# First four chunks of batch 0's q and k: from casting loads on GpSimd's queue to float32 loads on SyncE's queue with casts on chip

## The chip, the cores and the metric

The kernel runs on one core of a Trainium2 chip. The metric is device time in microseconds (us) of one execution. Before the change three runs took 257.55, 257.65 and 257.77 us (median 257.65). Shorter is better.

A core has a matmul engine (TensorE, PE in the profile), a vector engine (VectorE, DVE), an activation engine (ScalarE, ACT), GpSimd (POOL) and SyncE (SP). Sixteen DMA engines move data between memory and the core's on-chip buffer; SP, ACT and POOL issue to them, each through a queue of its own (in the profile q0 "software_dynamic" is POOL's, q1 SP's, q10 ACT's).

## The reference, cut to what matters

```python
qn = q / (np.linalg.norm(q, axis=1, keepdims=True) + 1e-06)      # q, k, v: 4 x 6400 x 256, float32
kn = k / (np.linalg.norm(k, axis=1, keepdims=True) + 1e-06)
s = kn.transpose(0, 2, 1) @ qn / tau                             # 256 x 256 for each batch
a = softmax(s)                                                   # over the last axis
x = v @ a                                                        # 25600 x 256
logits = x @ w_gate                                              # 8 experts, the best two of a row kept
out = x + sum over the two experts e of  w_e * (x @ A[e]) @ B[e] # rank 16
```

q, k, v and the output have 26.2 MB each. w_gate (8 KB), A (128 KB) and B (128 KB) are called the constants here.

## The kernel before, in words

For each of the 4 batches the kernel forms the 256 x 256 product of k and q ("gram", L194) and the sums of squares ("norm", L206, over squares made at L184 on ACT and L186 on DVE); a chain of seven short steps (`chain0` to `chain6`, L213 to L297) makes the softmax from them; then v is transposed and run through the softmax, the gate and the experts (L315 to L479). Batch 0's gram runs alone at the start (L491 to L500), then batch 0's chain (L501). From there one loop (L530 on) works in slots of two 128-row chunks of v, and the grams of batches 1 to 3 are dealt out over its slots. Each engine takes its instructions in the order written; nothing is rescheduled.

A batch has 50 chunks of 128 rows. q and k come in tiles `qk` of 10 chunks each (PC = 10, 4 buffers), v in tiles `vt` of 18, 16 and 16 chunks (3 buffers). All are loaded by POOL (L137, L138, L140), and these loads turn float32 into bfloat16 on the way. One partition's share of a 10-chunk load is 10 KB of float32 in one piece, so a load is 128 pieces, 8 for each of the 16 DMA engines. `load_more` (L119) issues the loads of a sorted list until the next tile's buffer is still in use; its argument limits how many tiles it takes. Before the gram it is called at L152 (three tiles), then the two identity matrices are made on POOL (L153 to L156), then at L163 (which gets one more tile, after which the four buffers are taken). The fifth tile of batch 0 comes in two parts, of 6 and 4 chunks.

SP loads the constants first (L149 w_gate, L150 A, L151 B; `wst`, `ast`, `bst`, float32). DVE casts them to bfloat16 at L168 to L171, before anything else that it does but three memsets. They are first used by batch 0's `chain5` (`wg_sb`, `A_sb`) and much later by L470 (`ball_sb`). SP has no other work until the last part of the kernel; most output is stored through ACT's queue (L488) out of tiles `ys`, of which there are 8 in rotation (L473).

The steps of the chain that the prediction touches, for batch 0: `chain2` ends with two multiplications on DVE (L243), `chain3` is the exponential on ACT (L251), `chain4` transposes it on PE (L263) and copies it out on DVE (L267), `chain5` multiplies it with the constants on PE (L279, L281).

Of the kernel before, what the change touches and what calls it, by code (L numbers as in the profile page):

```python
# [8 lines left out]
FP32 = mybir.dt.float32  # L9
BF16 = mybir.dt.bfloat16  # L10
# [6 lines left out]
def kernel(  # L17
# [16 lines left out]
    nc = tc.nc  # L34
    B, N, C = q.shape
    P = 128
    NC = N // P
    CC = C // P
    E = moe_w_gate.shape[1]
    R = moe_A.shape[2]  # L40
# [4 lines left out]
    PC = 10  # L45
    NPAIR = NC // 2
    NPT = B * NPAIR
    GRP = 5
    QKB, VB, YB = 4, 3, 8
    VP = [18, 16, 16]  # L50
    DEFER = 6

    GRAM = {1: (0, 20), 2: (24, 45), 3: (49, 67)}
# [2 lines left out]
    q_v = q.rearrange("b (p c) d -> b p c d", p=P)  # L56
    k_v = k.rearrange("b (p c) d -> b p c d", p=P)
# [3 lines left out]
    const = ctx.enter_context(tc.tile_pool(name="const", bufs=1))  # L61
# [4 lines left out]
    y_pool = ctx.enter_context(tc.tile_pool(name="yp", bufs=YB))  # L66
# [15 lines left out]
    for b, (first, last) in GRAM.items():  # L82
        n = last - first + 1
        for c in range(NC):
            s = first + c * n // NC
# [3 lines left out]

    loads = []  # L90
    for s in range(NC // PC):
        loads.append((-10 + s, "qk", 0, s, [PC] if s < NC // PC - 1 else [6, 4]))
        for b in range(1, B):
            loads.append((qk_need[b, s], "qk", b, s, [PC]))
    for b in range(B):
        for s, n in enumerate(VP):
            loads.append((NPAIR * b + sum(VP[:s]) // 2 + 1, "v", b, s,
                          [8, 4, 4] if b == B - 1 and s == len(VP) - 1 else [n]))
    loads.sort(key=lambda x: x[0])
    tiles = {"qk": {}, "v": {}}  # L100
    left = {"qk": [], "v": []}
# [4 lines left out]
    def piece(kind, c):  # L106
# [3 lines left out]
        s = 0  # L110
        while c >= VP[s]:
            c -= VP[s]
            s += 1
# [5 lines left out]
    def load_more(limit=1000):  # L119

        while limit and at_load[0] < len(loads):
            _, kind, b, s, parts = loads[at_load[0]]
            n = len(left[kind])
            if n >= bufs[kind] and left[kind][n - bufs[kind]]:
                return
            where[kind, b, s] = n
            left[kind].append(sum(parts))
            c0 = s * PC if kind == "qk" else sum(VP[:s])
            if kind == "qk":
                t = qk_pool.tile([P, 2, PC, C], BF16, tag="qk", name="qk")  # L130
            else:
                t = v_pool.tile([P, max(VP), C], BF16, tag="v", name="vt")
            tiles[kind][b, s] = t
            o = 0
            for m in parts:
                if kind == "qk":
                    nc.gpsimd.dma_start(t[:, 0, o:o + m, :], q_v[b, :, c0 + o:c0 + o + m, :])  # L137
                    nc.gpsimd.dma_start(t[:, 1, o:o + m, :], k_v[b, :, c0 + o:c0 + o + m, :])  # L138
                else:
                    nc.gpsimd.dma_start(t[:, o:o + m, :], v_v[b, :, c0 + o:c0 + o + m, :])  # L140
                o += m
            at_load[0] += 1
            limit -= 1


    wst = const.tile([P, CC * E], FP32)
    ast = const.tile([P, E, CC * R], FP32)
    bst = const.tile([P, C], FP32)
    nc.sync.dma_start(wst, moe_w_gate.rearrange("(p cc) e -> p (cc e)", p=P))  # L149
    nc.sync.dma_start(ast, moe_A.rearrange("e (p cc) r -> p e (cc r)", p=P))  # L150
    nc.sync.dma_start(bst, moe_B.rearrange("e r d -> (e r) d"))  # L151
    load_more(3)  # L152
    ident = const.tile([P, P], BF16)  # L153
    make_identity(nc, ident)
    ident_f = const.tile([P, P], FP32)
    make_identity(nc, ident_f)  # L156
    ones_bf = const.tile([P, 2], BF16)
    nc.vector.memset(ones_bf, 1.0)
    ones_f = const.tile([P, P], FP32)
    nc.vector.memset(ones_f, 1.0)  # L160
    neg_inv_tau = const.tile([P, 1], FP32)
    nc.vector.memset(neg_inv_tau, -inv_tau)
    load_more(3)  # L163

    wg_sb = const.tile([P, CC, E], BF16)
    A_sb = const.tile([P, CC, E, R], BF16)
    ball_sb = const.tile([P, C], BF16)
    nc.vector.tensor_copy(wg_sb.rearrange("p cc e -> p (cc e)"), wst)  # L168
    for cc in range(CC):
        nc.vector.tensor_copy(A_sb[:, cc, :, :], ast[:, :, cc * R:(cc + 1) * R])  # L170
    nc.vector.tensor_copy(ball_sb, bst)  # L171


    acc, nrm, sqs = {}, {}, {}
# [130 lines left out]
    for b in range(B):  # L305
        f = 0
# [174 lines left out]
    def send(keep):  # L481


        eng = nc.scalar if keep else nc.sync
        while len(unsent) > keep:
            gr = unsent.pop(0)
            c0, n = 2 * (gr["f"] - gr["b"] * NPAIR), 2 * gr["n"]
            eng.dma_start(out_v[gr["b"], :, c0:c0 + n, :], gr["ys"][:, 0:n, :])  # L488


    for c in range(0, NC, 2):  # L491
        square(0, c, "act" if (c // 2) % 2 else "dve")
        gram(0, c)
        gram(0, c + 1)
        load_more()
        if c >= 4:
            norm(0, c - 4)
            norm(0, c - 3)
    for c in range(NC - 4, NC):
        norm(0, c)  # L500
    for f, _ in CHAIN:  # L501
        f(0)

    def gram_part(items):
        for b, c in items:
            gram(b, c)
            if c >= 2:
                norm(b, c - 2)
            if c == NC - 1:
                norm(b, c - 1)  # L510
                norm(b, c)
# [18 lines left out]
    while nz < NPT or zq is not None or dq is not None:  # L530
# [4 lines left out]
        f, us, fb = (None, 0.0, 0) if behind else at_chain.get(slot, (None, 0.0, 0))  # L535
# [21 lines left out]
        dq, zq = zq, u  # L557
        send(max(0, min(DEFER, DEFER - (slot - GRAM[B - 1][1]) // 4)))
        if behind:
# [53 lines left out]
```

## Time and profile before

| | us |
|---|---|
| median of three runs | 257.65 |
| profiled execution, device time | 257.5 |
| its span in the profile | 255.7 |
| busy: PE / DVE / ACT / POOL | 215.5 / 150.6 / 174.9 / 30.9 |
| DMA: q0 (POOL's loads), time of its packets as a share of 16 engines' span | 75.3% |
| DMA: q10 (ACT's stores) / q1 (SP's) | 18.7% / 6.8% |
| read from memory / written | 78.91 MB / 26.21 MB |

The page cuts the span into 40 slices and gives each engine's busy tenths, the mean busy share of the DMA engines and what they moved. Its GB/s count bytes as they are written: a casting load writes half of what it reads, so 215 GB/s of q, k and v on chip are 430 GB/s read. The shares of DMA time add up the times of packets that overlap a little, so a full queue reads 1.03 to 1.1 and not 1.00. Other views used below: windows (busy time, DMA share and GB/s of chosen stretches), the timeline (instructions in order of time, with what ended the idle time before them in square brackets), the DMA view of a stretch (packets, MB and share of each queue), and the chain of waits that ended last.

### The profile page before, as it was taken

How to read it: one execution, taken by the hardware profiler on the slowest of the kernel's cores; microseconds unless marked ns; L12 is line 12 of the kernel's file. 1: busy time of each engine (PE TensorE's matmuls, PEld its weight loads, DVE VectorE, ACT ScalarE, POOL GpSimd, SP SyncE). 2: the span in 40 equal slices, each digit the busy share in tenths (PEclk: the TensorE clock that was granted, in tenths of full speed). 3: DMA queues.
4: the chain of work that ended last, by engine and by line, in shares of the span. 5: the costliest groups of instructions: out<-in, count | busy, mean ns of one | idle time of the engine just before them, and what ended most of it. 6: DMA issues, size and time to landing. Idle time of an engine off the chain costs nothing.

```text
span 255.7 us, 7679 instructions
## 1 busy us (share of the span) xinstructions
PE 215.5 (84%) x3256; PEld 191.1 (75%) x3256; DVE 150.6 (59%) x573; ACT 174.9 (68%) x288; POOL 30.9 (12%) x64
## 2 busy tenths in 40 slices
PE   0383884586899999999999989999899899999990
PEld 0262772475699987998999878989798789999970
DVE  1231333226386687775867857666577787777750
ACT  2333456449268778887888797887776877877881
POOL 8031131021012010210110202000000200000000
PEclk9997795589799999999999999999999999999998
DMA  7999999999999999999999999999999999999985
GB/s 122 219 214 214 211 215 219 210 216 215 214 218 213 220 209 216 216 214 214 215 218 210 288 269 289 218 307 256 284 261 269 372 342 352 383 424 425 421 368 210
DMA packets 12882, 66.29 MB, mean 259 GB/s; under 512 B 2480, under 2 KB 2608, under 8 KB 9008
## 3 DMA queue, kind: packets, MB, share of 16 engines
q0 software_dynamic: 8064, 39.33, 75.3%
q10 hardware_dynamic: 2160, 19.66, 18.7%
q1 hardware_dynamic: 2624, 6.82, 6.8%
q8 instruction: 25, 0.41, 0.6%
q14 instruction: 9, 0.07, 0.1%
HBM read 78.91 MB, written 26.21 MB: 411 GB/s over the span
## 4 chain that ended last, share of the span: by engine, by line
PE 47%; DMA 38%; DVE 7%; ACT 3%; issue 2%; POOL 1%; DVEq 0%; ACTq 0%; POOLq 0%
DMA qk<-in_k_dram 21%; PE y_ps L450 12%; DMA vt<-in_v_dram 11%; PE acc L194 8%; PE zg L434 6%; PE y_ps L470 6%; PE vT_ps L328 5%; DMA out_dram<-ys 5%; PE zg L458 3%; PE vT_ps L349 3%; PE nrm L206 3%; ACT sq L184 2%; DVE gz L438 2%; ACT ys L474 1%; DVE lm L384 1%
## 5 line engine op out<-in xcount | busy, mean ns | idle before, releaser
L184 ACT ACTIVATE sq<-qk 128x1024 bf16<-128x1024 bf16 x87 | 89.3, 1054 | 31.5 <-DMA qk<-in_k_dram 26.7
L194 PE MATMUL acc<-qk 128*128 128x256 bf16 x400 | 75.8, 292 | 19.9 <-DMA qk<-in_k_dram 19.9
L474 ACT COPY ys<-y_ps 128x512 f32<-128x512 f32 x100 | 58.7, 587 | 25.8 <-PE y_ps L470 21.8
L450 PE MATMUL y_ps<-a_bf,vT 128*128 128x256 bf16 x400 | 60.3, 273 | 0.3 <-ACT ys L474 0.3
L206 PEld LDWEIGHTS <-sq 128*128 128x128 bf16 x800 | 45.2, 99 | 8.5 <-ACT sq L184 3.1
L194 PEld LDWEIGHTS <-qk 128*128 128x128 bf16 x400 | 33.1, 102 | 23.7 <-DMA qk<-in_k_dram 20.8
L438 DVE TENSOR_TENSOR gz<-zg,gate 128x256 bf16<-128x256 f32 x100 | 41.6, 417 | 14.0 <-PE zg L434 12.4
L339 DVE COPY vT<-vT_ps 128x512 bf16<-128x512 bf16 x63 | 26.7, 423 | 34.3 <-PE vT_ps L328 33.6
L206 PE MATMUL nrm<-ones_bf,sq 128*128 128x1 bf16 x800 | 44.5, 165 | 1.2 <-ACT sq L184 1.2
L328 PE MATMUL vT_ps<-ident,vt 128*128 128x128 bf16 x400 | 39.5, 223 | 6.5 <-DMA vt<-in_v_dram 6.3
L434 PE MATMUL zg<-wa_sb,vT 128*128 128x128 bf16 x400 | 38.4, 218 | 1.2 <-DVE gzT L464 1.0
L470 PE MATMUL y_ps<-ball_sb,gzT 128*128 128x256 bf16 x200 | 38.4, 274 | 0.0
L328 PEld LDWEIGHTS <-vt 128*128 128x128 bf16 x400 | 29.9, 99 | 9.7 <-DMA vt<-in_v_dram 7.2
L450 PEld LDWEIGHTS <-vT 128*128 128x128 bf16 x400 | 33.5, 97 | 3.2 <-issue 0.4
L337 ACT COPY vT<-vT_ps 128x512 bf16<-128x512 bf16 x37 | 21.7, 587 | 10.2 <-PE vT_ps L328 8.7
L458 PE MATMUL zg<-ident,gz 128*128 128x128 bf16 x200 | 27.6, 220 | 1.1 <-DVE gz L438 0.6
L434 PEld LDWEIGHTS <-vT 128*128 128x128 bf16 x400 | 25.9, 96 | 3.4 <-issue 2.2
L464 DVE COPY gzT<-zg 128x256 bf16<-128x256 bf16 x90 | 25.2, 280 | 0.0
L137 POOL DMA_DIRECT2D qk<-in_q_dram x21 | 11.4, 542 | 111.8 <-ACT sq L184 31.8
L186 DVE TENSOR_TENSOR sq<-qk 128x1024 bf16<-128x1024 bf16 x13 | 8.9, 692 | 18.2 <-DMA qk<-in_k_dram 13.2
L458 PEld LDWEIGHTS <-gz 128*128 128x128 bf16 x200 | 15.0, 97 | 2.9 <-DVE gz L438 2.5
L470 PEld LDWEIGHTS <-gzT 128*128 128x128 bf16 x200 | 16.1, 98 | 0.4
(54 smaller groups left out, 150.7 us busy)
## 6 DMA issues: line engine op xcount, KB each, us to landing
out_dram<-ys ACTq DMA_DIRECT2D x15, 1280.0 KB, 13.1
qk<-in_q_dram POOLq DMA_DIRECT2D x19, 640.0 KB, 20.4
qk<-in_k_dram POOLq DMA_DIRECT2D x19, 640.0 KB, 23.9
vt<-in_v_dram POOLq DMA_DIRECT2D x7, 1024.0 KB, 28.6
out_dram<-ys SPq DMA_DIRECT2D x4, 1280.0 KB, 9.6
vt<-in_v_dram POOLq DMA_DIRECT2D x4, 1152.0 KB, 24.7
out_dram<-ys SPq DMA_DIRECT2D x5, 256.0 KB, 5.5
vt<-in_v_dram POOLq DMA_DIRECT2D x1, 512.0 KB, 11.1
```

Source lines behind the costliest of these rows:

```text
L184: nc.scalar.activation(sq, src, ACT.Square)
L194: nc.tensor.matmul(acc[b][:, ic, :], t[:, 1, o, ic * P:(ic + 1) * P], t[:, 0, o, :], start=(c == 0 and ic == 0), stop=(c == NC - 1), skip_ ...
L206: nc.tensor.matmul(nrm[b][:, j:j + 1], sq[:, w, c % 2, ic * P:(ic + 1) * P], ones_bf[:, 0:1], start=(c == 0 and j == 0), stop=(c == NC - 1 ...
L328: nc.tensor.matmul(pt[:, ic, sc * P:(sc + 1) * P], vt[:, o + sc, ic * P:(ic + 1) * P], ident, is_transpose=True, start=(i == 0), stop=(i = ...
L339: nc.vector.tensor_copy(dst, src)
L434: nc.tensor.matmul(z[:, sc, :], r["vT"][:, ic, sc, :], st[b]["wa"][:, ic, E:E + ER], start=(sc == 0 and ic == 0), stop=(sc == 1 and ic == ...
L438: nc.vector.tensor_tensor(out=gz.rearrange("p c (e r) -> p c e r", e=E), in0=z.rearrange("p c (e r) -> p c e r", e=E), in1=gr["gate"][:, r ...
L450: nc.tensor.matmul(y[:, sc, :], r["vT"][:, ic, sc, :], st[b]["a"][:, ic, :], start=(sc == 0 and ic == 0), stop=False, skip_group_check=True)
L458: nc.tensor.matmul(gt[:, sc, :], r["gz"][:, sc, :], ident, is_transpose=True, start=(sc == 0), stop=(sc == 1))
L464: nc.vector.tensor_copy(gzT, gt)
L470: nc.tensor.matmul(r["y"][:, sc, :], r["gzT"][:, sc, :], ball_sb, start=False, stop=(sc == 1), skip_group_check=True)
L474: nc.scalar.copy(gr["ys"][:, r["w"]:r["w"] + 2, :], r["y"])
```

## The change

1. A float32 tile `stage` (8 KB for a partition) is taken as the first of the rotating `ys` buffers. SP loads the first 4 chunks of batch 0's q and of its k into it, ahead of the constants.
2. POOL's first two loads bring only chunks 4 to 9 of the first tile.
3. The four chunks are cast to bfloat16 into the first `qk` tile: q's by DVE, k's by ACT, in two instructions of two chunks each.
4. SP's constants follow behind the two new loads, in the order w_gate, B, A (before: w_gate, A, B).
5. The fourth tile's loads are issued before the identity matrices are made, not after.
6. The casts of the constants leave DVE's start and are put behind batch 0's `chain3`, which is ahead of `chain4`'s copy L267 in DVE's order.

```diff
+    FIRST = 4
...
-        loads.append((-10 + s, "qk", 0, s, [PC] if s < NC // PC - 1 else [6, 4]))
+        loads.append((-10 + s, "qk", 0, s, {0: [PC - FIRST], NC // PC - 1: [6, 4]}.get(s, [PC])))
...
-            left[kind].append(sum(parts))
             c0 = s * PC if kind == "qk" else sum(VP[:s])
+            left[kind].append(PC if kind == "qk" else sum(parts))
+            o = left[kind][-1] - sum(parts)
...
-            o = 0
...
+    stage = y_pool.tile([P, 2 * GRP, C], FP32, tag="ys", name="stage")[:, 0:2 * FIRST, :].rearrange(
+        "p (w c) d -> p w c d", w=2)
+    nc.sync.dma_start(stage[:, 0, :, :], q_v[0, :, 0:FIRST, :])
+    nc.sync.dma_start(stage[:, 1, :, :], k_v[0, :, 0:FIRST, :])
...
     nc.sync.dma_start(wst, moe_w_gate.rearrange("(p cc) e -> p (cc e)", p=P))
+    nc.sync.dma_start(bst, moe_B.rearrange("e r d -> (e r) d"))
     nc.sync.dma_start(ast, moe_A.rearrange("e (p cc) r -> p e (cc r)", p=P))
-    nc.sync.dma_start(bst, moe_B.rearrange("e r d -> (e r) d"))
     load_more(3)
-    ident = const.tile([P, P], BF16)
-    make_identity(nc, ident)
-    ident_f = const.tile([P, P], FP32)
-    make_identity(nc, ident_f)
...
+    for c in range(0, FIRST, 2):
+        t = tiles["qk"][0, 0]
+        nc.vector.tensor_copy(t[:, 0, c:c + 2, :], stage[:, 0, c:c + 2, :])
+        nc.scalar.copy(t[:, 1, c:c + 2, :], stage[:, 1, c:c + 2, :])
+    load_more(1)
+    ident = const.tile([P, P], BF16)
+    make_identity(nc, ident)
+    ident_f = const.tile([P, P], FP32)
+    make_identity(nc, ident_f)
     load_more(3)
...
-    nc.vector.tensor_copy(wg_sb.rearrange("p cc e -> p (cc e)"), wst)
-    for cc in range(CC):
-        nc.vector.tensor_copy(A_sb[:, cc, :, :], ast[:, :, cc * R:(cc + 1) * R])
-    nc.vector.tensor_copy(ball_sb, bst)
+
+    def cast_constants():
+        nc.vector.tensor_copy(wg_sb.rearrange("p cc e -> p (cc e)"), wst)
+        for cc in range(CC):
+            nc.vector.tensor_copy(A_sb[:, cc, :, :], ast[:, :, cc * R:(cc + 1) * R])
+        nc.vector.tensor_copy(ball_sb, bst)
...
     for f, _ in CHAIN:
         f(0)
+        if f is chain3:
+            cast_constants()
```

## The prediction

> **What bounds the kernel now.** I read the windows first, cut where the work changes (columns: stretch, its length, busy time and count of PE, PEld, DVE, ACT, POOL, then PE's clock, the DMA share, GB/s written).
>
> ```profile
> 0.00:2.85 2.85, 0.00 (x0) 0.00 (x0) 0.41 (x4) 1.28 (x1) 1.82 (x7) 1.00 0.25 38
> 2.85:3.75 0.90, 0.00 (x0) 0.00 (x0) 0.00 (x0) 0.00 (x0) 0.90 (x3) 1.00 1.19 138
> 5.25:8.95 3.70, 0.00 (x0) 0.00 (x0) 0.00 (x0) 0.00 (x0) 1.36 (x4) 1.00 1.06 225
> 8.95:28.20 19.25, 12.12 (x144) 9.60 (x145) 5.55 (x9) 7.18 (x7) 3.71 (x7) 0.84 1.05 214
> 28.20:34.90 6.70, 5.70 (x98) 5.03 (x97) 2.52 (x5) 4.08 (x4) 1.58 (x3) 0.95 1.10 211
> 34.90:65.20 30.30, 18.77 (x272) 14.89 (x270) 11.16 (x38) 17.23 (x25) 4.76 (x9) 0.77 1.04 215
> 65.20:156.50 91.30, 89.28 (x1417) 80.68 (x1418) 65.46 (x251) 70.96 (x113) 11.64 (x23) 0.98 1.04 228
> 156.50:183.80 27.30, 25.92 (x414) 23.55 (x412) 17.89 (x65) 21.43 (x32) 1.59 (x3) 1.00 1.04 265
> ```
>
> The DMA engines are full from 2.85 us on and stay full. Until 65.2 us PE works 36.6 us of 62.35 and waits for loads; from 65.2 us PE is nearly full too. The chain of waits says the same: it runs through loads up to 65.20, then through PE.
>
> ```profile
> 1.89 8.86 DMA qk<-in_k_dram
> ...
> 17.60 18.70 DMA qk<-in_k_dram
> ...
> 36.58 28.58 DMA vt<-in_v_dram
> 65.20 0.40 PE vT_ps L328 x4
> ```
>
> So the end hangs on a load stream that never pauses. A shift of that stream moves 65.20, PE's stretch behind it and, the queue being still full, the loads that the chain waits for again from 156.5 to 183.8. I count a shift at 65.20 one for one at the end. Work on PE, ACT or DVE in batch 0 is worth nothing: PE stands idle for loads 3.3 us right before 65.20 and 2.7 us before 47.98.
>
> The start of the stream is the question. The timeline, then the DMA view of three stretches (queue: packets, MB, share; first 2.2 to 2.85 us, then 2.85 to 3.75, then 5.25 to 8.95):
>
> ```profile
> 0.74 0.38 SPq L149 DMA_DIRECT2D wst<-in_moe_w_gate_dram  x1
> 1.17 0.42 SPq L150 DMA_DIRECT2D ast<-in_moe_A_dram  x1
> 1.24 0.67 POOL L137 DMA_DIRECT2D qk<-in_q_dram  x1 [0.79 <-POOLq L594]
> ```
>
> ```profile
> q1 hardware_dynamic: 777, 0.10, 95.5%
> ```
>
> ```profile
> q0 software_dynamic: 18, 0.09, 95.6%
> q1 hardware_dynamic: 263, 0.03, 23.0%
> ```
>
> ```profile
> q0 software_dynamic: 153, 0.70, 93.1%
> q1 hardware_dynamic: 139, 0.13, 12.8%
> ```
>
> SP issues w_gate at 0.74; bytes move from 1.72 (first filled slice of the DMA view of 1.4 to 2.2), 0.98 us later. POOL issues q at 1.24; no q0 packet is seen before 2.85, 1.61 us later. Nearly all of A (1024 packets of 128 bytes) passes before POOL's stream begins, so it costs that stream almost nothing.
>
> **The change, part by part.**
>
> *Earlier start.* By the 1-us windows 1580 KB were written up to 10.00 us, 264 KB of them constants; 1316 KB at the steady 215 GB/s are 6.12 us, as if the stream began at 3.88. B, which comes inside the stream, takes 0.44 of that: 5.25:8.95 has 3.70 us, its 0.70 MB of q and k take 3.26 at 215 GB/s. Without B: 3.44. The first packet came at 2.85, so 0.59 us are lost to a slow start (138 GB/s in 2.85:3.75). After the change SP's q goes out at 0.74, its bytes by w_gate's row from 1.72. The slow start may come with being first (then it returns: 1.72 + 0.59 = 2.31, gain 1.1) or from A's small packets beside it (then it is gone: gain 1.7). Taken: 1.4, the middle. The bytes read are the same, at the same 430 GB/s.
>
> *The constants go into the full stream.* w_gate and A are 72 packets for each DMA engine that no longer pass in the idle stretch. Price: 777 packets in 0.65 us on 16 engines are 13 ns each; 72 make 0.9 us. Lower bound: their 139 KB alone at 430 GB/s, 0.3 us. Upper: B's packets in the full stream, 12.8% of 3.7 us over 139/16 packets, 54 ns each, of which 1 KB at 27 GB/s is 38; so 16 ns of overhead and 5 of bytes, 21 ns, 72 make 1.5 us. I take 0.9, the same packets' own rate. B is in the stream before and after: nothing.
>
> *Pieces of 4 and 6 KB for 10 KB.* 28.20:34.90 moved such pieces at 211 GB/s, 8.95:28.20 pieces of 10 KB at 214: 1.4% of 6 us, 0.1 us at most. Taken as nothing; upper end 0.26 (16 more packets of 16 ns).
>
> *The new casts.* DVE: 128 x 128 took 227 ns (L170's faster one) and 128 x 256 took 294 (L171), so 128 x 512 about 0.43; two. ACT: 128 x 512 in L474 587 ns; two. DVE and ACT wait there for data until 10.86 and 10.85. What stands behind these waiting casts is squares of the same tile. k's four chunks take turns with POOL's packets: 8 of 0.15 us and 8 of 0.23 from about 3 us, so they land near 7 and are cast by 8.3; the rest of the tile, 6.1 us of stream after 1.72, lands near 9 (before 10.80). Off the path, cost nothing; without that cover the load stream would still be the bound, since tile 2 lands no earlier than 15.
>
> *POOL's order.* The fourth tile's two loads (0.55 us each) pass ahead of 1.1 us of identity work. `ident_f` is first needed at 39.14. Nothing. The queue holds three tiles at that point, 18 us.
>
> *SP's order.* Two more issues, 0.38 to 0.57 us each; behind them only the constants, then nothing before the last stores.
>
> *The stage buffer.* The eighth group's `ys` waits for casts done near 8 us. The distance between stores in the rotation stays eight. Nothing.
>
> *The casts of the constants.* They take 0.18 + 0.53 + 0.29 = 1.00 us on DVE, in this gap:
>
> ```profile
> 41.07 0.75 DVE L243 TENSOR_TENSOR s_sb<-nrm,tk 128x256 f32<-128x256 f32 x2 [1.45 <-PE nrm L240]
> 43.21 0.42 DVE L267 COPY aT<-aT_ps 128x512 bf16<-128x512 bf16 x1 [1.39 <-PE aT_ps L263]
> ```
>
> 1.39 us idle; they end near 42.8, 0.4 before L267. Should they take 1 us longer, PE's 2.7 idle us before 47.98 still cover it. Their wait is new: w_gate, B and A must have landed. In 5.25:8.95 B's packets and POOL's go about one for one (139 to 153). One for one, SP's queue needs 97 turns from 2.85: half of q's, and 9, 9, 9 and 65 with their end marks. POOL's first 96 data packets for each engine are batch 0's q and k, over at 34.9. So A lands near 35, 6 us before DVE asks.
>
> Sum on the profiled execution: -1.4 + 0.9 = -0.5 us of 257.5 (span 255.7, 1.8 around it), 257.0. The median shown is 257.65, 0.15 above that execution; I subtract there: **257.15 us**. Bounds: -1.7 + 0.3 = -1.4 and -1.1 + 1.5 + 0.26 = +0.66.
>
> The Trainium skill's page "DMA: Bandwidth & Descriptors" speaks against the change in "Issuing engines are not separate DMA queues": issuing from several engines saves only the sequencer's time, usually small beside the transfer. Its specifications give a first byte after about 1 us from GpSimd and 0.6 us from SyncE, an estimated gain of 0.4 us where the rows above show 1.13 us between the first bytes; by the page the sum would be +0.5 us, 258.15. The same page ("Queues, rings and completion order") lets a DMA engine take a whole packet of some 9 to 17 descriptors from one ring before it turns to the next; by that A would be through in 4 to 7 turns and land before 20 us rather than near 35. B's row, one for one, stands nearer; both are in time.
>
> **The rivals.**
>
> *Small packets eat the gain, 257.85 (257.5 to 258.3).* The slow start comes again (gain 1.1) and 72 packets cost 16 to 21 ns (1.2 to 1.5). For it: B's 54 ns. Against it: shares in that stretch add to 106% as everywhere, so part of these times overlaps. Nothing is then gained, or 0.2 lost.
>
> *The constants come too late, 263 and more.* If SP's small packets get one turn for one and a half of POOL's, A lands after 145 of its packets: 96 until 34.9, then one tile of 16 (6.1 us), a v tile of 8 (5.4), 16 more (6.1) and 9 (3.4): near 56 us. DVE stands at the casts from 41.8, PE at L279 from 43.7. PE's work from there to 61.9 is 14.0 us; after the casts' 1 us it is done near 71 instead of by 65.2, so about +6. It decides from about 50 us, since PE has 7.5 idle us between 43.7 and 65.2; that is 1.34 turns for one. Against it: the 139 to 153.
>
> *The stream's start doesn't count, 257.65.* If the shift is lost to PE's clock or order of buffers after 65.2, nothing remains. For it: PE is 98% busy from 65.2 to 156.5. Against: PE's start there waits for the load itself.
>
> **How the numbers follow.** Forecast, gain of 0.2 to 1.4 us: 0.60. Eaten gain: 0.22. Shift lost: 0.10. Late constants: 0.08. About 0.2% (0.5 us) is what a measurement of this kernel tells from no change. Of the forecast 0.49 lies beyond it and 0.11 within; of the eaten gain 0.12 within and 0.10 slower, its upper part and unforeseen delays; the lost shift is half within, half slower (0.05 each); late constants 0.08 slower. Faster 0.49, same 0.28, slower 0.23. The range, 256.3 to 258.2, spans the bounds of the sum and leaves out the late constants and the outermost of the rest.
>
> **What would show it.** In the profile after: q1 moves about 0.5 MB from 1.7 us at full share; the first gram near 8 instead of 10.80; L328's wait that ended at 65.20 ends 0.2 to 1.4 earlier, and the end by as much; GB/s between 9 and 28 us under 214, from A's packets. DVE's casts of constants after 41 us start at once, not on a DMA. Wrong if that cast waits for `ast`, or if 65.20 moves and the end doesn't.

## The result and the profile after

| | before | after |
|---|---|---|
| median, us (8 runs each; lowest to highest) | 257.68 (257.45 to 257.88) | 256.94 (256.60 to 257.48) |
| profiled execution, us | 257.5 | 256.87 |
| its span | 255.7 | 255.1 |
| wait for v that ended at 65.20 before | 65.20 | 64.52 |

The changed kernel is faster by 0.74 us; the ratio is 0.9975, 95% interval 0.9966 to 0.9985. The forecast was 257.15. A ratio, here and below, counts only those runs of a kernel that lie within 1.5% of its fastest.

The windows of the changed kernel, first cut by single microseconds at the start, then by the stages of before (columns as above; SP's new loads are float32 and written whole, so that a full queue writes 430 GB/s here and not 215):

```profile
1.00:2.00 1.00, 0.00 (x0) 0.00 (x0) 0.04 (x2) 1.00 (x1) 0.77 (x2) 1.00 0.37 49
2.00:3.00 1.00, 0.00 (x0) 0.00 (x0) 0.00 (x0) 0.01 (x1) 1.00 (x3) 1.00 0.76 229
3.00:4.00 1.00, 0.00 (x0) 0.00 (x0) 0.00 (x0) 0.00 (x0) 1.00 (x3) 1.00 0.99 373
4.00:5.00 1.00, 0.00 (x0) 0.00 (x0) 0.57 (x2) 0.00 (x0) 1.00 (x3) 1.00 1.05 401
8.95:28.20 19.25, 14.35 (x156) 10.85 (x156) 4.84 (x7) 6.34 (x6) 3.75 (x7) 1.00 1.09 216
28.20:34.90 6.70, 5.50 (x61) 4.22 (x62) 2.07 (x3) 3.17 (x3) 1.06 (x2) 1.00 1.15 217
34.90:64.52 29.62, 19.68 (x286) 15.77 (x285) 11.99 (x42) 18.23 (x25) 5.33 (x10) 0.80 1.04 215
64.52:156.50 91.98, 89.94 (x1412) 81.32 (x1413) 65.28 (x251) 70.90 (x113) 11.52 (x22) 0.97 1.04 228
156.50:183.24 26.74, 25.88 (x415) 23.78 (x414) 18.03 (x66) 21.59 (x32) 1.73 (x4) 1.00 1.04 267
```

The first bytes come near 1.75 us, so most of the first row is empty. By 3.00 us 0.28 MB have come, which at the full rate take 0.65 us and here took 1.25; from 3 us the rate is nearly full (373 and 401 GB/s). From there the picture is that of before: the queue is full, PE waits for loads until 64.52, works nearly without a pause behind it, and near the end waits for loads again. The chain of waits, before and then after, shows this last load of k:

```profile
156.49 27.20 DMA qk<-in_k_dram
```

```profile
156.63 26.50 DMA qk<-in_k_dram
```

It landed at 183.69 before and at 183.13 after, 0.56 us earlier (183.35 in the second execution of the changed kernel, after_again below); the wait for v ended 0.68 us earlier, and the span is 0.6 shorter. So the last load that the end waits for carries the shift too.

The first instructions of the timeline that matter, and the places that the prediction named:

```profile
0.74 0.37 SPq L150 DMA_DIRECT2D stage<-in_q_dram  x1
1.16 0.43 SPq L151 DMA_DIRECT2D stage<-in_k_dram  x1
...
4.43 0.90 DVE L167 CAST qk<-stage 128x512 bf16<-128x512 f32 x2 [3.39 <-DMA stage<-in_q_dram]
...
5.72 1.14 ACT L168 CAST qk<-stage 128x512 bf16<-128x512 f32 x2 [3.70 <-DMA stage<-in_k_dram]
...
6.39 1.89 PE L207 MATMUL acc<-qk 128*128 128x256 bf16 x8 [6.39 <-ACT qk L168]
...
9.86 1.04 PE L207 MATMUL acc<-qk 128*128 128x256 bf16 x4 [1.58 <-DMA qk<-in_k_dram]
...
41.91 0.17 DVE L181 CAST wg_sb<-wst 128x16 bf16<-128x16 f32 x1
41.98 0.35 DVE L183 CAST A_sb<-ast 128x128 bf16<-128x128 f32 x2
42.25 0.29 DVE L184 CAST ball_sb<-bst 128x256 bf16<-128x256 f32 x1
43.38 0.42 DVE L280 COPY aT<-aT_ps 128x512 bf16<-128x512 bf16 x1 [0.85 <-PE aT_ps L276]
...
64.52 0.61 PE L341 MATMUL vT_ps<-ident,vt 128*128 128x128 bf16 x4 [3.11 <-DMA vt<-in_v_dram]
```

The first gram starts at 6.39 instead of 10.80, but it runs out of data at once and waits for the rest of the tile until 9.86. The constants' casts carry no bracket: they start without a wait, right behind the multiplication before them, and DVE is idle again for 0.85 us before L280.

Where the time came from is read off the bytes. The DMA view of the first 10 us, before (queue: packets, MB, share; q0 is POOL's queue, whose MB are bfloat16 as written, so half of what it reads; q1 is SP's):

```profile
q0 software_dynamic: 275, 1.31, 69.0%
```

The first 33 us, before:

```profile
q0 software_dynamic: 1518, 6.19, 94.1%
```

The first 10 us, after:

```profile
q0 software_dynamic: 330, 1.00, 50.5%
q1 hardware_dynamic: 569, 1.18, 37.5%
```

The first 33 us, after:

```profile
q0 software_dynamic: 1587, 5.79, 86.9%
q1 hardware_dynamic: 1616, 1.32, 16.3%
```

By 10 us the kernel before had read 2 x 1.31 = 2.62 MB of q and k. After, it is 2 x 1.00 plus SP's 1.05 MB (2 x 4 chunks of 131 KB), 3.05 MB. The lead of 0.43 MB is 1.0 us at 430 GB/s. By 33 us it is 12.38 MB against 11.58 + 1.05 = 12.63: 0.25 MB, 0.58 us. So in this execution the earlier start gains 1.0 us, and A, which passes meanwhile, takes 0.4 back. One execution isn't the measure of the first figure: the profiles of five experiments below that start in the same way have a lead of 0.7 to 0.95 us at 10 us (after_again: 2 x 0.97 + 1.05 MB, 0.86 us, of which 0.40 are left at 33 us). What A takes, 0.4 to 0.5 us, agrees between the two executions of the changed kernel.

### The profile page after: what moved, and what is told of

Same layout as the page of the kernel before. It is cut to its first block, busy times and chain, and to the rows that moved or that the text cites. A ratio compares the mean times of both kernels' runs of the same rounds, so it can differ in the third digit from the quotient of the medians.

```text
span 255.1 us, 7688 instructions
## 1 busy us (share of the span) xinstructions
PE 221.0 (87%) x3256; PEld 194.4 (76%) x3256; DVE 151.2 (59%) x575; ACT 176.5 (69%) x290; POOL 31.6 (12%) x64
## 4 chain that ended last, share of the span: by engine, by line
PE 48%; DMA 36%; DVE 7%; ACT 3%; POOL 2%; issue 2%; DVEq 0%; ACTq 0%; POOLq 0%
DMA qk<-in_k_dram 20%; PE y_ps L463 12%; DMA vt<-in_v_dram 11%; PE acc L207 8%; PE zg L447 6%; PE y_ps L483 6%; DMA out_dram<-ys 5%; PE vT_ps L341 5%; PE zg L471 3%; PE vT_ps L362 3%; PE nrm L219 3%; ACT sq L197 2%; DVE gz L451 2%; POOL qk L138 1%; ACT ys L487 1%
## 5 line engine op out<-in xcount | busy, mean ns | idle before, releaser
L207 PE MATMUL acc<-qk 128*128 128x256 bf16 x400 | 81.5, 310 | 15.2 <-DMA qk<-in_k_dram 8.8
L219 PEld LDWEIGHTS <-sq 128*128 128x128 bf16 x800 | 46.9, 102 | 10.1 <-ACT sq L197 3.2
L207 PEld LDWEIGHTS <-qk 128*128 128x128 bf16 x400 | 34.6, 106 | 20.3 <-DMA qk<-in_k_dram 10.0
L219 PE MATMUL nrm<-ones_bf,sq 128*128 128x1 bf16 x800 | 45.2, 166 | 1.2 <-ACT sq L197 1.2
```

The lines of the kernel that those rows point to most:

```text
L207: nc.tensor.matmul(acc[b][:, ic, :], t[:, 1, o, ic * P:(ic + 1) * P], t[:, 0, o, :], start=(c == 0 and ic == 0), stop=(c == NC - 1), skip_ ...
L219: nc.tensor.matmul(nrm[b][:, j:j + 1], sq[:, w, c % 2, ic * P:(ic + 1) * P], ones_bf[:, 0:1], start=(c == 0 and j == 0), stop=(c == NC - 1 ...
```

## The experiments

Twelve runs of experiments, one of them the changed kernel again, each set against the kernel before on the same chip. The theory was: the end follows the load stream one for one; the stream gains 1.0 us at its start and pays some 0.4 to 0.5 us for the constants, 7 ns for a packet and not 13. Its rivals were that the gain has another source (the moved casts, POOL's order), that the packets are dear and the start worth more, and that the shift of the stream isn't what counts.

| kernel | median us | ratio to before, 95% | wait for v ends | profiled time less that |
|---|---|---|---|---|
| before | 257.68 | | 65.20 | 192.30 |
| after | 256.94 | 0.9975 (0.9966 to 0.9985) | 64.52 | 192.35 |
| after_again | 256.76 | 0.9971 (0.9960 to 0.9982) | 64.94 | 192.15 |
| rest_alone | 257.70 | 1.0000 (0.9991 to 1.0008) | 65.23 | 192.50 |
| pool_undone | 257.11 | 0.9979 (0.9970 to 0.9989) | 64.52 | 192.54 |
| cast_early | 263.77 | 1.0240 (1.0227 to 1.0253) | 71.56 | 192.39 |
| a_three | 257.88 | 1.0006 (0.9997 to 1.0014) | 65.50 | 192.55 |
| a_rows | 256.86 | 0.9969 (0.9957 to 0.9980) | 64.45 | 192.41 |
| k_act | 256.91 | 0.9969 (0.9957 to 0.9981) | 64.95 | 192.24 |
| const_act | 256.84 | 0.9968 (0.9956 to 0.9980) | 64.51 | 192.55 |
| const_first | 258.83 | 1.0029 (1.0006 to 1.0051) | 70.65 | 192.02 |
| first2 | 257.78 | 1.0010 (0.9992 to 1.0028) | 65.79 | 191.63 |
| first3 | 256.82 | 0.9974 (0.9961 to 0.9986) | 65.31 | 191.80 |
| first5 | 257.10 | 0.9980 (0.9971 to 0.9989) | 64.83 | 192.27 |

The last two columns come from one profiled execution each. Two executions of the changed kernel differ there by 0.4 us (64.52, 64.94), so a shift below that is read from the medians and the bytes. In first3 the wait ends even later than before (65.31 against 65.20), and the kernel is faster all the same (ratio 0.9974).

### Is it the early loads at all? rest_alone, pool_undone, after_again

rest_alone is the kernel before with the fourth tile ahead of the identities and the constants' casts in the softmax, and no float32 loads:

```diff
     load_more(3)
+    load_more(1)
...
+        if f is chain3:
+            cast_constants()
```

> The kernel before with two parts of the change and without the float32 loads: the constants' casts moved into batch 0's softmax and the fourth tile issued ahead of the identities. Theory (the gain is the stream's earlier start): 257.7, as before. Rival (the moved casts or the order on GpSimd's queue bring the gain, or a part of it): 256.9 to 257.3.

257.70 us, ratio 1.0000: these two parts bring nothing by themselves.

pool_undone is the changed kernel with the identities ahead of the fourth tile again; after_again is the changed kernel a second time, beside it.

```diff
-    load_more(1)
```

> The changed kernel with the fourth tile's loads behind the identities again, as before the change. The queue holds three tiles at that point, so nothing changes: 256.9. Rival (the order on GpSimd's queue carries a part of the gain): 257.2 or more.

> The changed kernel again, as the measure for the three runs beside it: 256.9, spread some 0.9 us as in its first eight runs.

257.11 and 256.76 us; the intervals overlap (0.9970 to 0.9989, 0.9960 to 0.9982). The means differ by 0.2 us, and by the spread of the runs anything from 0 to 0.5 fits: a gain from POOL's order beside the early loads is neither shown nor excluded.

### Do the moved casts matter? cast_early

The changed kernel with the constants' casts back at DVE's start:

```diff
+    cast_constants()
...
-        if f is chain3:
-            cast_constants()
```

> The changed kernel with the constants' casts back at VectorE's start, behind the stage casts. If A lands near 31 us (the profile after), VectorE stands there until then, TensorE at the first norms, the first tile's buffer comes free only after that, and GpSimd's queue runs dry at about 27 us; without its packets the rest of A goes quickly, so VectorE goes on near 28, the fifth tile is issued near 31 and the stream misses some 4 us: 260 to 263. Rival (where the casts stand matters little, the load stream covers it): 257.

263.77 us, 6.8 above the changed kernel and a little above the 260 to 263 expected. The timeline of this run, DVE's and POOL's lines:

```profile
28.81 0.36 DVE L183 CAST A_sb<-ast 128x128 bf16<-128x128 f32 x2 [20.72 <-DMA ast<-in_moe_A_dram]
...
32.88 0.56 POOL L138 DMA_DIRECT2D qk<-in_q_dram  x1 [26.18 <-ACT sq L199]
```

And its windows:

```profile
26.00:28.81 2.81, 0.00 (x0) 0.00 (x0) 0.00 (x0) 0.00 (x0) 0.00 (x0) 1.00 0.78 150
29.00:34.00 5.00, 3.96 (x47) 3.09 (x48) 2.88 (x7) 1.35 (x2) 1.11 (x3) 1.00 0.00 0
```

The cast waits 20.7 us for A, and behind it in DVE's order stand the squares of batch 0. All four `qk` buffers fill meanwhile; none comes free, POOL can't issue the fifth tile before 32.88, and from 29 to 34 us not a byte is loaded (DMA share 0.00). The wait for v then ends at 71.56, 7.0 us later than in the changed kernel, and the profiled time is 7.1 us longer (263.95 against 256.87). This is the strongest row for "one for one at the end", and it shows what the moved casts are: worth nothing alone, and the condition without which the rest costs 6.8 us.

### What do the constants cost? a_three, a_rows

a_three loads A two more times behind the first, into a spare part of the float32 tile that nothing reads:

```diff
+    for i in range(2):
+        nc.sync.dma_start(whole[:, 2 * FIRST + i, :].rearrange("p (e r) -> p e r", e=E),
+                          moe_A.rearrange("e (p cc) r -> p e (cc r)", p=P))
```

> A is loaded three times in all (two more copies into unused parts of the stage tile; nothing reads them): 128 more packets of 128 bytes for each DMA engine, in turns with the full stream. The prediction's price of 13 ns a packet gives +1.7 us over the changed kernel (256.9), so 258.6. The price that the profile after suggests (the lead of q's and k's bytes falls from 1.0 us at 10 us to 0.5 at 33 us, 6 to 7 ns a packet) gives +0.85, so 257.8. If small packets cost nothing but hide beside large ones: 256.9.

257.88 us, 0.94 over the changed kernel's median, or 0.80 by the two ratios, each taken on its own chip, for 128 more packets on each DMA engine: 6 to 7 ns for one. The DMA view says the same. From 33 to 95 us, the changed kernel's POOL queue:

```profile
q0 software_dynamic: 2581, 13.22, 104.0%
```

and a_three's two queues:

```profile
q0 software_dynamic: 2571, 13.06, 102.3%
q1 hardware_dynamic: 1897, 0.24, 4.9%
```

POOL's loads write 0.16 MB less, so 0.32 MB less is read, 0.74 us at 430 GB/s, for 1897 / 16 = 119 packets: 6 ns. The bytes of a 128-byte packet alone are 4.7 ns at a DMA engine's 27 GB/s (430 / 16). So small packets inside a full stream cost little more than their bytes; 13 ns is refuted.

a_rows brings A in 128 pieces of 1 KB instead of 1024 of 128 bytes.

```diff
-    nc.sync.dma_start(ast, moe_A.rearrange("e (p cc) r -> p e (cc r)", p=P))
+    nc.sync.dma_start(ast.rearrange("p e r -> p (e r)"), moe_A.rearrange("e (q s) r -> (e q) (s r)", s=16))
```

> A is loaded as 128 pieces of 1 KB and not 1024 of 128 bytes: the same bytes, 8 packets for each DMA engine instead of 64. It lands in another order, so the experts' matrix is a permuted one and the output another. At 13 ns a packet beyond its place (the prediction's price): 56 packets less, -0.5 to -0.7 us, 256.3. At the 6 to 7 ns of the run with A three times, of which some 4.7 are the bytes themselves: -0.1, 256.8.

A's rows then lie in another order on chip, so the experts' matrix is a permuted one and the output another; the kernel serves for its time alone.

256.86 us: 56 packets fewer on each engine gain nothing that can be measured, where 13 ns each would have given 0.7 us. The bytes agree: the lead of q and k, worked out as above, falls from 0.95 us at 10 us to 0.53 at 15 us, while A's 8 larger packets pass on each engine, and stays there until 33 us. So A takes 0.4 us of the stream in 8 packets as in 64; its 131 KB alone are 0.3 us at 430 GB/s.

### What is the slow start? k_act, const_act

k_act sends k's float32 load through ACT's queue beside q's on SP:

```diff
-    nc.sync.dma_start(stage[:, 1, :, :], k_v[0, :, 0:FIRST, :])
+    nc.scalar.dma_start(stage[:, 1, :, :], k_v[0, :, 0:FIRST, :])
     (ACT's table load, before at the kernel's start, behind it)
```

> The float32 load of k goes through ScalarE's queue at 0.7 us (its table load behind it), q's through SyncE's. If the slow start is one ring working through its first packets one by one, two rings fill the engines sooner: 256.5. If it is on the memory side, whoever is first pays it: 256.9, and the first packets take twice as long.

256.91 us. Its windows:

```profile
1.00:2.00 1.00, 0.00 (x0) 0.00 (x0) 0.04 (x2) 0.82 (x1) 0.76 (x2) 1.00 0.43 57
2.00:3.00 1.00, 0.00 (x0) 0.00 (x0) 0.00 (x0) 0.46 (x1) 1.00 (x3) 1.00 0.68 180
3.00:4.00 1.00, 0.00 (x0) 0.00 (x0) 0.00 (x0) 0.00 (x0) 1.00 (x3) 1.00 0.98 369
```

57, 180, 369 GB/s, where the changed kernel has 49, 229, 373 and, in its second execution, 45, 160, 401: two queues start no faster than one. The slow start isn't that of one queue; what it is, no run here shows.

const_act sends the constants through ACT's queue at the start, ahead of its table load:

```diff
-    nc.sync.dma_start(wst, ...
-    nc.sync.dma_start(bst, ...
-    nc.sync.dma_start(ast, ...
+    nc.scalar.dma_start(wst, ...
+    nc.scalar.dma_start(bst, ...
+    nc.scalar.dma_start(ast, ...
     (ACT's table load behind them)
```

> The constants go through ScalarE's queue at the start (its table load behind them), q's and k's float32 loads alone on SyncE's. If the small packets pass beside the slow start of q's first packets, where the DMA engines are not full (0.37 and 0.76 of 1 in the second and third us), their 0.5 us are saved in part: 256.4 to 256.7. Rival: they cost the same wherever they stand, or slow the start itself: 256.9 or more.

256.84 us, no difference to the changed kernel, so the 256.4 to 256.7 were missed. The constants don't slip into an idle stretch for free here. In the window of 2 to 3 us,

```profile
2.00:3.00 1.00, 0.00 (x0) 0.00 (x0) 0.00 (x0) 0.86 (x1) 1.00 (x3) 1.00 0.50 132
```

132 GB/s are written, at a DMA share of 0.50. That the constants are paid for in the slow start of q and k fits this row, but doesn't follow from it: executions that start as the changed kernel does show 152 (a_three) to 229 GB/s there.

### Must q and k go first? const_first

The two float32 loads behind the three constants on SP:

```diff
-    nc.sync.dma_start(stage[:, 0, :, :], q_v[0, :, 0:FIRST, :])
-    nc.sync.dma_start(stage[:, 1, :, :], k_v[0, :, 0:FIRST, :])
     (w_gate, B, A)
+    nc.sync.dma_start(stage[:, 0, :, :], q_v[0, :, 0:FIRST, :])
+    nc.sync.dma_start(stage[:, 1, :, :], k_v[0, :, 0:FIRST, :])
```

> The constants go first on SyncE's queue again, the float32 loads of q and k behind them; the casts of the constants stay in batch 0's softmax. If the gain is that q's bytes fill the first idle stretch, it is lost but for the constants' own passage: 257.4 to 257.7. Rival: the gain comes from another part (the moved casts, the earlier work on the first four chunks, the order on GpSimd's queue): it stays at 256.9.

Median 258.83 us, and the twelve runs lie between 257.39 and 264.15. Three of them, over 262 us, aren't in the ratio, which is 1.0029 without them: no gain is left, so the rival's 256.9 is out, and the time is even a little longer than the 257.4 to 257.7 expected. The profiled one is one of the three, 262.67 us. Its timeline:

```profile
2.10 0.58 SPq L156 DMA_DIRECT2D stage<-in_q_dram  x1
...
21.82 0.76 DVE L167 CAST qk<-stage 128x512 bf16<-128x512 f32 x2 [20.79 <-DMA stage<-in_q_dram]
...
26.20 1.14 ACT L168 CAST qk<-stage 128x512 bf16<-128x512 f32 x2 [24.18 <-DMA stage<-in_k_dram]
...
31.42 0.56 POOL L138 DMA_DIRECT2D qk<-in_q_dram  x1 [24.73 <-PE nrm L219]
```

q's load is issued at 2.10 and its data are cast at 21.82, 19.7 us later. The DMA view of 5 to 6 us, then of 6 to 17:

```profile
q1 hardware_dynamic: 717, 0.09, 61.6%
q0 software_dynamic: 55, 0.12, 61.5%
```

```profile
q0 software_dynamic: 483, 1.99, 89.0%
q1 hardware_dynamic: 471, 0.68, 19.3%
```

Most of A's 1024 packets pass in one microsecond, many to one of POOL's. What is left of A, and q and k behind it, then passes one for one with POOL's packets by their number (471 to 483). The stream runs dry as in cast_early: no buffer is free until 31.42. The theory had priced only the lost gain; the new wait was in neither expectation. How much of A passes in that first burst would explain the scatter, but the short executions were not profiled, so that is argued only.

### How many chunks? first2, first3, first5

```diff
-    FIRST = 4
+    FIRST = 2        # and 3, and 5 (there the last cast takes one chunk alone)
```

> Two chunks of q and k by SyncE instead of four (256 KB each). If only the moment counts at which full-size packets begin, and GpSimd's packets are ready by 2.85 us as in the kernel before, they take over when SyncE's run out near 3.5: 256.9. Rival: GpSimd's first packet came at 4.7 in the changed kernel; if that is its own delay and not the others' turn, the engines stand idle for about 1 us: 257.7 or more.

> Three chunks by SyncE. Two chunks gave 257.8 with runs from 256.8 to 259.4, and the profile's tiles landed up to 2 us later although as many bytes had moved. Theory: with little ahead of it GpSimd's stream takes the DMA engines over while they are still in the slow start, not all at once, and a tile is there only when the last engine has brought its part; three chunks then stand between, 257.0 to 257.5 with a wider spread than four. Rival (the two-chunk run was a bad draw of the chip): 256.9.

> Five chunks by SyncE. If all that counts is that full-size packets begin early and last until GpSimd's are ready on every engine, nothing more is gained: 256.9. If more float32 on SyncE's queue were better for itself (fewer pieces for GpSimd), 256.7 or less. If the constants, now later still, or the longer casts hurt: 257.1 or more.

257.78, 256.82 and 257.10 us. Three to five chunks can't be told apart: three lose nothing, and five gain nothing more. Two chunks lose the whole gain, in one series of runs with a wide spread (256.77 to 259.43), and the cause stays open; that this series was a bad draw isn't excluded. The median is what was expected if POOL's stream were late by a delay of its own, but that isn't the reason: its first packet comes near 3.3 us here, and not at 4.7. In the timeline the first two tiles are late:

```profile
12.11 1.89 PE L207 MATMUL acc<-qk 128*128 128x256 bf16 x8 [4.64 <-DMA qk<-in_k_dram]
...
18.33 1.03 PE L207 MATMUL acc<-qk 128*128 128x256 bf16 x4 [2.01 <-DMA qk<-in_k_dram]
```

They wait until 12.11 and 18.33, where the changed kernel waits until 9.86 and 16.13. Yet the bytes of the first 10 us,

```profile
q0 software_dynamic: 316, 1.20, 63.3%
q1 hardware_dynamic: 541, 0.64, 22.6%
```

are 2.40 MB by POOL and 0.52 of SP's, 2.92 against 2.62 before and 3.05 after. So the bytes are 0.7 us ahead of the kernel before and the first tile is 1.3 us behind it (12.11 against 10.80). By 33 us the lead is gone:

```profile
q0 software_dynamic: 1529, 5.94, 90.1%
```

With SP's 0.52 that is 12.40 MB against 12.38 before, which fits a median as before. A load has landed when all of its 128 pieces have, so it can be late although as many bytes have moved; whether some DMA engines fell behind, and why with two chunks only, no run tells apart.

## Why the prediction was right, and where not

- **The stream bounds the kernel, one for one at the end: right.** 64.45 to 71.56 us for the wait, and the profiled time less the wait stays at 191.6 to 192.6. For the 0.7 us of the change itself, medians, bytes and the last load of k say it; the wait in a single pair of profiles wouldn't be enough.
- **Earlier start, forecast 1.4 us: too large, 1.0 by the bytes at 10 us, and 0.7 to 0.95 in five other profiles that start so.** The forecast took the middle of 1.1 (the slow start comes back for whoever is first) and 1.7 (it was due to A's small packets). It came back: 0.28 MB by 3.00 us, some 0.6 us behind the full rate that the sign expected from the first byte on; and the first bytes did come near 1.7. All six leads lie under the lower of the two figures.
- **Constants in the full stream, forecast 0.9 us: twice what they took.** A's packets lie between 9.9 and 31.4 us. In the stretch of 10 to 31.5 us POOL's queue, before,

```profile
q0 software_dynamic: 1099, 4.57, 104.8%
```

  and both queues after:

```profile
q0 software_dynamic: 1086, 4.47, 102.0%
q1 hardware_dynamic: 1046, 0.14, 7.5%
```

  show 0.10 MB less written, 0.20 MB less read, 0.47 us for A's 64 packets: 7 ns, as a_three. The 13 ns came from a stretch in which those packets were alone. In the full stream their own time is 7.5% of 21.5 us, 1.6 us on each engine, and the stream loses only 0.47 of them: the rest lies beside the time of POOL's packets.
- **The sum, -0.5 us: right, partly because two errors cancel.** 1.0 - 0.4 = 0.6 by the bytes, 0.74 measured (0.4 to 0.9 by the interval). The sum fell 0.2 us short; of its two terms one was 0.4 too large and the other 0.5. That they nearly cancel is luck.
- **One for one turns, A near 35 us: right.** 1046 packets of SP's to 1086 of POOL's, and A through by 31.4 us, 10 us before DVE asks. It was a little earlier since q's and most of k's packets passed before POOL's stream began and took no turns with it. The Trainium skill's page "DMA: Bandwidth & Descriptors" ("Queues, rings and completion order") has an engine drain some 9 to 17 descriptors of one ring before it switches; the measurement decides, and in the full stream it was one against one. At the start of a stream it wasn't: 717 to 55 in const_first, and 263 to 18 in the second DMA view of the prediction.
- **New casts, first gram near 8 us: beside the path as said, with other times.** k's four chunks don't take turns with POOL's packets, since POOL has none yet: from 2.85 to 4.6 us the DMA view lists SP's queue alone,

```profile
q1 hardware_dynamic: 178, 0.66, 98.4%
```

  and the gram starts at 6.39. Even with the turns, the prediction's own 8 x 0.15 + 8 x 0.23 from 3 us end at 6.0 and not near 7. The rest of the tile lands at 9.86 (forecast 9), as POOL's stream begins later than in the kernel before.
- **GB/s under 214 between 9 and 28 us: a badly chosen sign.** It is 216, because SP's constants are in that figure too. POOL's own bytes between 9 and 28 us do fall, from 4.05 to 3.95 MB.
- **POOL's order, SP's order, the smaller pieces, the stage buffer: nothing,** as rest_alone bears out for POOL's order without the early loads; no run sets the others apart. The moved casts gain nothing, but cast_early shows that nothing covers them if they stay in place. The prediction didn't price that.
- **The rivals.** "Small packets eat the gain" was right that the slow start comes again, but its 16 to 21 ns for a packet fail by a_three's 6 to 7; "the stream's start doesn't count" by cast_early and the medians. "Constants too late" didn't happen, but its price was of the right size: where a cast does wait for A, it costs 6.8 us. It does so by the buffers of batch 0 and not by `chain5`, so the agreement is chance.
- **The estimate from the Trainium skill.** Its page "DMA: Bandwidth & Descriptors" ("Issuing engines are not separate DMA queues") says that starting DMAs on several engines saves only the sequencer's time. k_act agrees: a second queue for k makes no difference (256.91 against 256.94). The change gained more: 0.7 to 1.0 us by the bytes, where SP issues its first load of q 0.50 us before POOL did (0.74 against 1.24). The 258.15 came from the first-byte figures of the page's "Specifications" and left these 0.50 us out; with them the same estimate is a gain of 0.9 us and 257.65. Measured was 256.94.

## What to carry to other kernels

In a kernel bound by a load stream that never pauses, the first microseconds are part of the bound: let the queue whose first bytes come soonest carry the first data that count, and put small transfers behind them. Then look at who waits for those small ones: beside a full queue they advanced one packet a turn, so what stood behind them in their queue (const_first), and the engine that asked for them early (cast_early), waited some 20 us. A packet's cost should be read from a stretch in which it shares the engines, not from one in which it is alone.

## What the runs showed of the hardware that had not been expected

- The slow start comes with the first large transfer, whichever queue carries it: 0.28 MB by 3.00 us with q and k both by SP (0.21 in after_again), 0.24 with q by SP and k by ACT. In the kernel before it came with POOL's first load, 138 GB/s in 2.85 to 3.75 us, although SP's constants had moved already.
- With SP's large packets queued first, POOL's first packet comes at 4.7 us, though POOL issued its load at 1.23; before, it issued at 1.24 and the packet came at 2.85. It is no fixed delay: with 2, 3, 4 and 5 chunks ahead the packet comes near 3.3, 4.1, 4.7 and 5.5 us, and a chunk of q and of k is 0.26 MB, 0.61 us at 430 GB/s. In the changed kernel SP's queue had the engines to itself from 2.85 to 4.6 us, and the one-for-one turns began only after that.
- A small load inside a full stream is cheap for the stream (6 to 7 ns for a 128-byte packet, and A as a whole 0.4 us in pieces of 128 bytes or of 1 KB) and dear for whoever waits for it: A's load takes 29.4 us from issue to landing, where it took 2.9 us in the kernel before.
